# A fused attention and mixture-of-experts kernel: row counts, scatter and expert choice placed in the next step, squares at the step's end, q and k in one tile

## The chip, the cores and the metric

The kernel runs on one core of a Trainium2 chip. The metric is the device time of one execution in microseconds; the time given is the median of three runs. One further execution was taken by the hardware profiler, and all rows below come from it.

The core's engines run side by side, each in its own fixed order, and wait for one another on semaphores. PE does the matrix products (its weight loads are the row PEld), DVE and ACT work on tiles elementwise, POOL issues the indirect transfers (scatters) and SP issues the plain ones.

## What is computed

The reference computes a channel attention over four batches of 5056 tokens with 256 channels, and passes its output, as 20224 rows, through a mixture of eight experts of which each row uses one.

```python
qn = q / (np.linalg.norm(q, axis=1, keepdims=True) + 1e-06)
kn = k / (np.linalg.norm(k, axis=1, keepdims=True) + 1e-06)
s = kn.transpose(0, 2, 1) @ qn / tau            # 256 x 256 for each batch
a = softmax(s);  x = v @ a
...
logits = x @ w_gate + modality_bias[modality_id]
e_idx = np.argmax(logits, axis=1)
for e in range(E):                              # 8 experts, 256 -> 1024 -> 256
    mask = e_idx == e
    h = np.maximum(x[mask] @ w1[e], 0.0)
    out[mask] = gate_w[mask, None] * (h @ w2[e])
```

The norms run over the tokens, so a batch's `a` is known only when all of its q and k have been read. An expert's rows are known only as the routing goes on.

## The kernel before

**Steps.** The tokens are taken in steps of 512 (the last step of a batch has 448), ten to a batch, 40 in all, numbered `g`. In step `g`, three streams of pieces are merged by `_interleave`, which takes from each in proportion to its length:

- `va_pieces(g)`: the transposes `vtp` of the next step's v, their halves `vh` and `vl`, the products `xp` = v·a with their copies into `x` (L543), and then `route`;
- `kq_pieces(b + 1, s)`: loads of q and k of the next batch, halves `qs` and `ks` (L298, L299), squares and their sums for the norms (L322, L324), and the matmuls `g` = kᵀq (L343);
- `block_pieces`: one block of 512 rows of one expert, with weight halves (L722, L729), transposed rows `xtp`, `xh`, `xl`, the first layer `hp` with `hh` and `hl`, the second layer `y`, and `yo` with its scatter to the output.

Products are done in split precision: a value is kept as a high and a low half, and three products are summed. For batch 0 and the first five steps of batch 1 `g` uses whole values.

**Routing.** `route` (L547 to L608) adds the bias, finds each row's best expert as a one-hot tile `oh`, counts rows with a running sum `run`, and multiplies both with triangular and all-one matrices on PE: the three matmuls `rp` (L575 to L577). From `rp`, DVE forms the new counts `bs` (L582), each row's position `pos`, and the row numbers `pi` (L591). POOL then scatters the four tiles of `x` to their experts' places in the DRAM tensor `xs` (L454).

**Expert choice.** `pick` (L620 on) takes the counts `bs` of a step and chooses on DVE which expert has the next full block; SP loads the result `pki` into registers and uses it in the addresses of the block's weights (L701, L705) and rows (`xr`, L682). A block starts four steps after its choice (fewer after step 12); the first is chosen at step 2 and starts at step 6. There are 40 blocks, numbered by `slot`.

**What sets the order.** The program is written in the order in which the pieces are called; a scheduler then orders each engine's instructions by that and by the buffers (`p1`, `p2`, `p3`, `p4` are pools with 1 to 4 buffers per tag). Some orders are given by hand: `order(ins, others)` puts an instruction behind others of its engine, and in batch 0 the halves and squares of q and k are put behind `routed[g - 1]`, the last routing instructions of the step before. SP issues its loads in order, so a load that waits for a buffer holds those behind it. Names such as `filler1` are unused tiles that place other tiles in memory.

Of the kernel before, what the change touches and what calls it, by code (L numbers as in the profile page):

```python
# [34 lines left out]
def kernel(  # L35
# [216 lines left out]
    filled = []  # L252
    acc = {}

    def kq_pieces(b, s, behind=(), later=None):
# [11 lines left out]
        def load():  # L267
            if s == 0:
                gram[b] = ps1.tile([P, CH, C], F32, tag="y0" if b == 0 else "g", name=f"g_{b}")
                acc[b] = p1.tile([P, 2, 2 * C], F32, tag="acc", name=f"acc_{b}", bufs=2)  # L270
                if b == 0:
                    p1.tile([P, 48], F32, tag="filler2", name="filler2")
            for n, src, tag in (("q", q, "w1r"), ("k", k, "w2r")):
                if (b == 0 and s % 5 >= 2) or (b == 1 and 2 <= s < START + 2):
                    st[n] = p3.tile([P, TT, C], F32, tag=tag, name=f"{n}_{b}_{s}")
                else:
                    st[n] = p2.tile([P, TT, C], F32, tag=n, name=f"{n}_{b}_{s}")
                rows = src[b, t0 : t0 + pp * TT, :].rearrange("(p t) c -> p t c", t=TT)
                if b == 0 and s == 0:
                    st[n + "rows"] = rows  # L280
                else:
                    nc.sync.dma_start(st[n][:pp], rows)
            if b == 0 and s == 0:
                for h in range(2):
                    ts = slice(2 * h, 2 * h + 2)
                    for n in ("q", "k"):
                        nc.sync.dma_start(st[n][:, ts, :], st[n + "rows"][:, ts, :])

        def split(h):
            ts = slice(2 * h, 2 * h + 2)  # L290
            whole = s in WHOLE[b]
            more = h == 1 and (b == 0 or (b == 1 and s < START + 1))
            if not whole:
                st["q", h] = p2.tile([P, 2, 2 * C], F32R, tag="xh" if more else "qs", name=f"qs_{b}_{s}_{h}")
                st["k", h] = p2.tile([P, 2, 2 * C], F32R, tag="xl" if more else "ks", name=f"ks_{b}_{s}_{h}")
# [11 lines left out]
        def square(h):  # L307
            ts = slice(2 * h, 2 * h + 2)
            a = acc[b]
            for n, o in (("q", 0), ("k", C)):  # L310
                first = h == 0 and s == 0
                sq = a[:, :, o : o + C]
                if not first:
                    if b == 0 and s == 0 and n == "q":
                        p3.tile([P, 80], F32, tag="filler5", name="filler5", bufs=1)
                    if b == 0 and n == "k" and not filled:
                        filled.append(p3.tile([P, 48], F32, tag="filler1", name="filler1", bufs=1))
                    if b == 0 or (b == 1 and s < AHEAD):
                        sq = p3.tile([P, 2, C], F32, tag="hh" if n == "q" else "hl", name=f"sq_{b}_{s}_{h}_{n}")
                    else:  # L320
                        sq = p2.tile([P, 2, C], F32, tag="sq", name=f"sq_{b}_{s}_{h}_{n}")
                act(nc.scalar.activation(sq[:pp], st[n][:pp, ts, :], AF.Square))  # L322
                if not first:
                    dve(nc.vector.tensor_tensor(a[:pp, :, o : o + C], a[:pp, :, o : o + C], sq[:pp], ALU.add))  # L324

        def mm(h):
            for t in range(2):
                first = s == 0 and h == 0 and t == 0
                last = s == NS - 1 and h == 1 and t == 1
                for m in range(CH):  # L330
                    ms = slice(m * P, (m + 1) * P)
                    if s in WHOLE[b]:
                        seq = [(st["k"][:pp, 2 * h + t, ms], st["q"][:pp, 2 * h + t, :])]
                    else:
                        ks, qs = st["k", h], st["q", h]
                        lo = slice(C + m * P, C + (m + 1) * P)
                        seq = [
                            (ks[:pp, t, ms], qs[:pp, t, 0:C]),
                            (ks[:pp, t, ms], qs[:pp, t, C : 2 * C]),
                            (ks[:pp, t, lo], qs[:pp, t, 0:C]),  # L340
                        ]
# [16 lines left out]
    def softmax_pieces(b):  # L358
        st = {}

        def norms():
            a = acc[b]
            ns = ps2.tile([P, 512], F32, tag="aux", bufs=3, name=f"ns_{b}")
            for h in range(2):
                nc.tensor.matmul(
                    ns[:, 0:C], ones, a[:, h, 0:C], start=h == 0, stop=h == 1, skip_group_check=True
                )
            for m in range(CH):
                for h in range(2):
                    nc.tensor.matmul(  # L370
                        ns[:, C + m : C + m + 1], a[:, h, C + m * P : C + (m + 1) * P], ones[:, 0:1],
# [113 lines left out]
    def va_pieces(b, s):  # L485
# [59 lines left out]
        def route():  # L545
# [20 lines left out]
            W = TT * E  # L566
# [4 lines left out]
            if early:  # L571
# [39 lines left out]
            fetch,  # L611
        )
# [8 lines left out]
    def pick(g, slot, tail):  # L621

        nc.vector.tensor_copy(end9[:, 0:E], bases[g])
        n = 3 if tail else 2
# [16 lines left out]
        nc.vector.tensor_scalar(rem, rem, m, None, ALU.is_equal)  # L641
        nc.vector.tensor_tensor(pr[:, 0, :], rem, nxt9, ALU.mult)
        nc.vector.tensor_tensor(pr[:, 1, :], rem, eid9, ALU.mult)
# [3 lines left out]
        nc.vector.tensor_reduce(pk[:, 0:n], pr[:, 0:n, :], AX.X, ALU.add)  # L647
# [25 lines left out]
    def block_pieces(g, slot, picked, tail):  # L673
        pki, padded = picked
# [4 lines left out]
        def load_x():  # L679
            r = nc.sync.value_load(pki[0:1, 0:1], min_val=0, max_val=E * CAP)  # L680
# [14 lines left out]
        def load_w(hf):  # L695
            if hf == 0:
                st["e"] = nc.sync.value_load(pki[0:1, 1:2], min_val=0, max_val=E - 1)
# [13 lines left out]
        def split_w(ci):  # L711
            a, c = st["wr"][ci // 2]
            o = ci % 2
            if slot == 0 and ci == 0:
                p4.tile([P, 64], F32, tag="filler3", name="filler3", bufs=1)
# [36 lines left out]
        def m1(j):  # L752
# [8 lines left out]
            for i, (w, x, h) in enumerate(seq):  # L761
                nc.tensor.matmul(hp[:, 0:rows], w[:, h, fs], x[:, h, 0:rows], start=i == 0, stop=i == len(seq) - 1)  # L762
            hh = p3.tile([P, BLK], F32R, tag="hh", name=f"hh_{slot}_{j}")
            hl = p3.tile([P, BLK], F32R, tag="hl", name=f"hl_{slot}_{j}")
# [112 lines left out]
    squares = {1: [], 2: []}  # L877
    for s in BEFORE:
        if s == 0:
            run(kq_pieces(1, s))  # L880
        else:
            run(kq_pieces(1, s, lambda: routed[0], squares[s]))
    pad_rows()
    for g in range(G):
# [12 lines left out]
        streams.append(soft + (va[g + 1][0] if g + 1 < G else []) + va[g][1])  # L897
        if b + 1 < B:
            if b == 0 and s == 1:
                streams.append(list(kq_pieces(1, 2, lambda: routed[1], squares[2])))  # L900
            else:
                streams.append([f for i in (PLAN[s] if b == 0 else [s]) for f in kq_pieces(b + 1, i, routed[g - 1] if b == 0 and g > 0 else ())])
        _interleave(*streams)
        run(squares.get(g + 1, []))
# [3 lines left out]
        if s == NS // 2 and b < B - 1:  # L908
            setup_bias(b + 1, routed[g])
        n = slots_by(g)  # L910
# [87 lines left out]
```

## Time and profile before

| | |
|---|---|
| median of three runs | 1247.93 us (1247.73 to 1249.01) |
| the profiled execution's own time | 1241.93 us |
| span from first to last instruction of it | 1240.2 us |
| mean granted TensorE clock | 0.997 |
| bytes read, written | 167.06 MB, 43.43 MB |

Rows of the profile give the line of the kernel, the engine, the operation, the tile written and the tiles read, and then busy time or waits. A wait is the idle time of an engine just ahead of an instruction, with what released it. PE's clock is given as a share of full speed.

### The profile page before, as it was taken

To read this page: it belongs to the slowest core of one execution; us is meant where nothing else is said; L and a number is where in the kernel's file an instruction comes from. 1 tells how busy PE (TensorE), PEld (TensorE's weight loads), DVE (VectorE), ACT (ScalarE), POOL (GpSimd) and SP (SyncE) were. 2 spreads that over 40 slices of the span, in tenths; PEclk is the share of its full clock that TensorE was granted. 3 is DMA by queue.
4 is the path that set the end of the run, shared out by engine and by line. 5 is a ranking of instruction groups with operands and counts; after the bars stand their busy time and mean duration, and the time that the engine had idled before them with its cause. 6 is when DMAs were issued, how large, how long until landed. Compare 5 with 4: busy or idle time off the path is not lost. (4 is left out here: it accounts for less than half of the span.)

```text
span 1240.2 us, 23781 instructions
## 1 busy us (share of the span) xinstructions
PE 1215.5 (98%) x8368; PEld 1116.8 (90%) x8368; DVE 829.3 (67%) x2182; ACT 736.7 (59%) x1511; POOL 365.1 (29%) x344
## 2 busy tenths in 40 slices
PE   8989999999999999999999999999999999999997
PEld 7878898999999999998999999999899999989997
DVE  6789687767667776776677776656555665575552
ACT  6656667766666666675666666556455555545552
POOL 0053342223232333312333323322322233333121
PEclk9999999999999999999999999999999999999999
DMA  8979565455555565545555554444554454443430
GB/s 309 297 236 298 161 200 174 156 171 177 185 184 171 172 182 184 178 143 165 178 181 188 154 185 152 147 131 138 174 165 137 148 162 149 126 145 123 147 98 29
DMA packets 104177, 210.83 MB, mean 170 GB/s; under 512 B 11336, under 2 KB 52808, under 8 KB 104048
## 3 DMA queue, kind: packets, MB, share of 16 engines
q1 hardware_dynamic: 88304, 167.61, 43.5%
q0 software_dynamic: 15744, 41.61, 9.0%
q8 instruction: 67, 1.10, 0.4%
q14 instruction: 62, 0.51, 0.1%
HBM read 167.06 MB, written 43.43 MB: 170 GB/s over the span
## 5 line engine op out<-in xcount | busy, mean ns | idle before, releaser
L454 POOL DMA_INDIRECT xs<-x,pi x160 | 179.5, 1122 | 681.5 <-ACT w1h L722 302.3
L780 PE MATMUL y<-w2h,hh 128*128 128x256 f32 x1264 | 357.6, 283 | 1.8 <-issue 0.9
L780 PE MATMUL y<-w2l,hh 128*128 128x256 f32 x1264 | 352.6, 279 | 0.1
L780 PE MATMUL y<-w2h,hl 128*128 128x256 f32 x1264 | 350.9, 278 | 0.1
L766 DVE SCALAR_TENSOR_TENSOR hl<-hp,hh 128x512 fp32r<-128x512 f32 (+1 forms) x320 | 216.4, 676 | 67.8 <-ACT hh L765 61.4
L762 PE MATMUL hp<-xh,w1h 128*128 128x512 f32 (+1 forms) x640 | 254.4, 398 | 0.0
L762 PE MATMUL hp<-xh,w1l 128*128 128x512 f32 (+1 forms) x640 | 250.3, 391 | 0.0
L762 PE MATMUL hp<-xl,w1h 128*128 128x512 f32 (+1 forms) x640 | 249.9, 391 | 0.0
L780 PEld LDWEIGHTS y<-w2h,hh 128*128 128x128 f32 x1264 | 237.5, 188 | 13.1 <-ACT yo L796 1.9
L780 PEld LDWEIGHTS y<-w2l,hh 128*128 128x128 f32 x1264 | 238.0, 188 | 10.1 <-issue 0.5
L765 ACT ACTIVATE hh<-hp 128x512 fp32r<-128x512 f32 (+1 forms) x320 | 190.3, 595 | 82.6 <-PE hp L762 75.7
L780 PEld LDWEIGHTS y<-w2h,hl 128*128 128x128 f32 x1264 | 236.7, 187 | 0.5 <-DVE hl L766 0.3
L729 DVE TENSOR_TENSOR w1l<-w1r,w1h 128x512 fp32r<-128x512 f32 x160 | 110.2, 689 | 179.4 <-ACT w1h L722 171.3
L454 POOL DMA_INDIRECT out_dram<-yo,xr x158 | 171.7, 1087 | 158.0 <-ACT yo L796 121.4
L722 ACT CAST w1h<-w1r 128x512 fp32r<-128x512 f32 x160 | 100.1, 626 | 142.9 <-PE hp L762 130.1
L762 PEld LDWEIGHTS hp<-xh,w1l 128*128 128x128 f32 x640 | 120.1, 188 | 26.0
L762 PEld LDWEIGHTS hp<-xl,w1h 128*128 128x128 f32 x640 | 120.4, 188 | 14.7 <-issue 0.4
L762 PEld LDWEIGHTS hp<-xh,w1h 128*128 128x128 f32 x640 | 120.1, 188 | 12.7
L722 ACT CAST w2h<-w2r 128x512 fp32r<-128x512 f32 x160 | 101.0, 631 | 48.4 <-PE y L780 45.8
L729 DVE TENSOR_TENSOR w2l<-w2r,w2h 128x512 fp32r<-128x512 f32 x160 | 110.2, 689 | 25.3 <-ACT w2h L722 23.2
L543 ACT COPY x<-xp 128x264 f32<-128x264 f32 x160 | 61.2, 383 | 91.2 <-PE xp L539 67.5
L539 PE MATMUL xp<-ah,vh 128*128 128x264 f32 x320 | 93.1, 291 | 0.4 <-issue 0.4
(146 smaller groups left out, 1710.4 us busy)
## 6 DMA issues: line engine op xcount, KB each, us to landing
w1r<-in_moe_w_dram SPq DMA_DIRECT2D x80, 512.0 KB
w2r<-in_moe_w_dram SPq DMA_DIRECT2D x80, 512.0 KB
xr<-xs SPq DMA_DIRECT2D x38, 516.0 KB
v<-in_v_dram SPq DMA_DIRECT2D x36, 512.0 KB
q<-in_q_dram SPq DMA_DIRECT2D x35, 512.0 KB
k<-in_k_dram SPq DMA_DIRECT2D x35, 512.0 KB
xs<-x,pi POOLq DMA_INDIRECT x160
out_dram<-yo,xr POOLq DMA_INDIRECT x158
```

The costliest lines, as they stand in the source:

```text
L454: ins = nc.gpsimd.indirect_dma_start(out=dst, out_offset=bass.IndirectOffsetOnAxis(ap=idx, axis=0), in_=rows, in_offset=None, bounds_check ...
L539: nc.tensor.matmul(xp[:, 0:DE], a[:, h, t * P : (t + 1) * P], w[:, h, :], start=i == 0, stop=i == len(seq) - 1,)
L543: nc.scalar.copy(st["x"][:, t, :], xp[:, 0:DE])
L722: ins = nc.scalar.copy(hi, src).ins
L729: nc.vector.tensor_tensor(lo, src, hi.bitcast(F32), ALU.subtract)
L762: nc.tensor.matmul(hp[:, 0:rows], w[:, h, fs], x[:, h, 0:rows], start=i == 0, stop=i == len(seq) - 1)
L765: nc.scalar.activation(hh[:, 0:rows], hp[:, 0:rows], AF.Relu)
L766: nc.vector.scalar_tensor_tensor(hl[:, 0:rows], hp[:, 0:rows], 0.0, hh[:, 0:rows].bitcast(F32), ALU.max, ALU.subtract)
L780: ins = nc.tensor.matmul(y, a[:, tsl], w[:, j % 2, :], start=(j == 0 and i == 0 and t % 2 == 0), stop=(j == NJ - 1 and i == 2), skip_group ...
```

## The change

It has three parts.

1. The end of `route` becomes a function of its own, `place`: the `rp` matmuls, `bs`, `pos`, `pi` and the scatter. It is put into the stream of the next step, behind that stream's first two pieces, and the expert choice `pick` is called right behind it. A block's `picked` list is made at once and filled then. Only the last step keeps both in itself.
2. The squares of q and k and their sums are collected in a list `late` and run when the step's streams have been merged, except those of a batch's last step. The hand-written orders behind `routed` fall away for them.
3. q and k share a tile `qk` of 2 x 4 x 256 columns per partition, and their halves share `qkh` and `qkl`, so that copies, subtractions, squares and sums run over 1024 columns instead of twice 512. The two weight matrices of a half block share a tile `w` as well. `pick` forms its sums with the products, by `accum_out`, instead of by a reduction behind them.

```diff
         def split(h):
+            src = st["qk"][:pp, :, 2 * h : 2 * h + 2, :]
...
-            for n in () if whole else ("q", "k"):
-                t = st[n, h]
-                act(nc.scalar.copy(t[:pp, :, 0:C], st[n][:pp, ts, :]))
-                dve(nc.vector.tensor_tensor(
-                    t[:pp, :, C : 2 * C], st[n][:pp, ts, :], t[:pp, :, 0:C].bitcast(F32), ALU.subtract
-                ))
+            if s not in WHOLE[b]:
...
+                act(nc.scalar.copy(hi[:pp], src))
+                dve(nc.vector.tensor_tensor(lo[:pp], src, hi[:pp].bitcast(F32), ALU.subtract))
...
         def square(h):
...
-                act(nc.scalar.activation(sq[:pp], st[n][:pp, ts, :], AF.Square))
-                if not first:
-                    dve(nc.vector.tensor_tensor(a[:pp, :, o : o + C], a[:pp, :, o : o + C], sq[:pp], ALU.add))
+            act(nc.scalar.activation(sq[:pp], src, AF.Square))
+            if not first:
+                dve(nc.vector.tensor_tensor(a[:pp], a[:pp], sq[:pp], ALU.add))
...
             nc.vector.tensor_tensor_scan(rtf, keep, ohf, 0.0, ALU.mult, ALU.add)
-            if early:
+            st["routing"] = (oh, run_t, ex)
+
+        def place():
...
+            if g < first_block - 1:
                 rp = ps1.tile([P, 512], F32, tag="y0", name=f"rp_{g}")
             else:
                 rp = ps2.tile([P, 512], F32, tag="aux", bufs=3, name=f"rp_{g}")
...
-        nc.vector.tensor_scalar(rem, rem, m, None, ALU.is_equal)
-        nc.vector.tensor_tensor(pr[:, 0, :], rem, nxt9, ALU.mult)
-        nc.vector.tensor_tensor(pr[:, 1, :], rem, eid9, ALU.mult)
-        if tail:
-            nc.vector.tensor_tensor(pr[:, 2, :], rem, pr[:, 2, :], ALU.mult)
+        nc.vector.tensor_tensor(rem, rem, m.to_broadcast([P, E + 1]), ALU.is_equal)
         pk = p2.tile([P, 3], F32, tag="pk", name=f"pk_{slot}")
-        nc.vector.tensor_reduce(pk[:, 0:n], pr[:, 0:n, :], AX.X, ALU.add)
+        for i, x in enumerate((nxt9, eid9) + ((pr[:, 2, :],) if tail else ())):
+            nc.vector.scalar_tensor_tensor(
+                pr[:, 0, :], rem, 1.0, x, ALU.mult, ALU.mult, accum_out=pk[:, i : i + 1]
+            )
...
-            a = p3.tile([P, CH, FH], F32, tag="w1r", name=f"w1r_{slot}_{hf}")
-            c = p3.tile([P, JH, D], F32, tag="w2r", name=f"w2r_{slot}_{hf}")
+            w = p3.tile([P, 2, JH * D], F32, tag="w", name=f"w_{slot}_{hf}")
...
+    def placed(g):
+
+        def choose(slot, picked):
+            picked.extend(pick(g, slot, False))
+
+        return [va[g][3]] + [lambda p=p: choose(*p) for p in picks.get(g, [])]
...
-        streams.append(soft + (va[g + 1][0] if g + 1 < G else []) + va[g][1])
+        turns = va[g + 1][0] if g + 1 < G else []
+        own = soft + turns + va[g][1] + (placed(g) if g == G - 1 else [])
+        if g > 0:
+            own[2:2] = placed(g - 1)
+        streams.append(own)
+        late = []
...
+                for f in kq_pieces(b + 1, i, later=None if i == NS - 1 else late)
+            ])
         _interleave(*streams)
-        run(squares.get(g + 1, []))
+        run(squares.get(g + 1, []) + late)
```

The next rows show how PE's order changes in three places. First, PE around the counts of step 2, ahead of the first block, in the kernel before (`xp_3_0` is the first row tile of step 3, `g_1` the product for batch 1):

```order
L521 MATMUL vtp_4_0_864<-ident_79,v_4_854 128x128 x4
L539 MATMUL xp_3_0_884<-ah_0_440,vh_3_746 128x264
...
L521 MATMUL vtp_4_1_877<-ident_79,v_4_854 128x128 x4
L539 MATMUL xp_3_0_884<-ah_0_440,vl_3_747 128x264
L343 MATMUL g_1_483<-q_1_3_860,k_1_3_862 128x256 x3
L575 MATMUL rp_2_811<-oh_2_807,trim_95 128x32
L576 MATMUL rp_2_811<-run_2_809,onesb_88 128x32
L577 MATMUL rp_2_811<-run_2_809,onesb_88 128x8
L343 MATMUL g_1_483<-q_1_3_860,k_1_3_862 128x256
L539 MATMUL xp_3_1_896<-ah_0_440,vh_3_746 128x264
```

The same place in the changed kernel:

```order
L572 MATMUL rp_1_640<-run_1_619,onesb_88 128x8
L332 MATMUL g_1_413<-qk_1_3_728 128x256 x2
L528 MATMUL xp_3_0_791<-ah_0_370,vh_3_629 128x264
...
L528 MATMUL xp_3_3_815<-ah_0_370,vh_3_629 128x264
L570 MATMUL rp_2_738<-oh_2_718,trim_95 128x32
L528 MATMUL xp_3_3_815<-al_0_371,vh_3_629 128x264
...
L571 MATMUL rp_2_738<-run_2_720,onesb_88 128x32
L572 MATMUL rp_2_738<-run_2_720,onesb_88 128x8
L332 MATMUL g_1_413<-qk_1_3_728 128x256 x2
L510 MATMUL vtp_5_0_857<-ident_79,v_5_848 128x128 x4
```

The matmuls of `rp_2` stood behind the first row tile of step 3, and now its first stands behind the first matmul of the fourth; those of `rp_1` stand ahead of step 3.

Second, PE at the end of step 9, the last of batch 0, before (`hp_3_7` is the last chunk of block 3's first layer):

```order
L762 MATMUL hp_3_7_3025<-xl_3_2399,w1h_3_3_2797 128x512
L575 MATMUL rp_9_2997<-oh_9_2993,trim_95 128x32
L762 MATMUL hp_3_7_3025<-xh_3_2398,w1l_3_3_2798 128x512
L576 MATMUL rp_9_2997<-run_9_2995,onesb_88 128x32
L577 MATMUL rp_9_2997<-run_9_2995,onesb_88 128x8
L343 MATMUL g_1_483<-qs_1_9_1_2950,ks_1_9_1_2951 128x256 x12
L780 MATMUL y0_3_2752<-w2h_3_2_2725,hh_3_5_2887 128x256
```

And in the changed kernel, where `rp_9` stands in block 4:

```order
L757 MATMUL hp_4_1_2923<-xh_4_2709,w1h_4_0_2652 128x512
...
L779 MATMUL y0_3_2577<-w2h_3_3_2625,hh_3_7_2810 128x256
...
L779 MATMUL y1_3_2578<-w2h_3_3_2625,hl_3_7_2811 128x256
L570 MATMUL rp_9_2960<-oh_9_2825,trim_95 128x32
L571 MATMUL rp_9_2960<-run_9_2827,onesb_88 128x32
L572 MATMUL rp_9_2960<-run_9_2827,onesb_88 128x8
L757 MATMUL hp_4_2_3040<-xh_4_2709,w1h_4_1_2795 128x512
```

It moved behind the 12 `g` of the last q and k, three groups of `y` and two groups of `hp`.

Third, PE at the start of the first block, before:

```order
L539 MATMUL xp_5_3_1196<-ah_0_440,vl_5_991 128x264
L743 MATMUL xtp_0_0_1259<-identr_84,xr_0_1152 128x128 x4
L743 MATMUL xtp_0_1_1260<-identr_84,xr_0_1152 128x128 x4
L521 MATMUL vtp_7_0_1378<-ident_79,v_7_1124 128x128 x4
L762 MATMUL hp_0_0_1329<-xh_0_1257,w1h_0_0_1248 128x512
```

And in the changed kernel:

```order
L332 MATMUL g_1_413<-qkl_1_5_1_1418,qkh_1_5_1_1417 128x256
L332 MATMUL g_1_413<-qkh_1_5_1_1417,qkl_1_5_1_1418 128x256
L738 MATMUL xtp_0_0_1123<-identr_84,xr_0_1002 128x128 x4
L738 MATMUL xtp_0_1_1124<-identr_84,xr_0_1002 128x128 x4
L510 MATMUL vtp_7_0_1215<-ident_79,v_7_976 128x128 x3
L757 MATMUL hp_0_0_1176<-xh_0_1121,w1h_0_0_1112 128x512
```

The 24 matmuls `g` of batch 1's step 5 stand ahead of the block's row transposes `xtp` now; before, they stood inside the block.

More of the change, by code (lines that the diff above doesn't have):

```diff
@@ L251 @@
     gram = {}
-    filled = []
     acc = {}
@@ L269, in load @@
                 gram[b] = ps1.tile([P, CH, C], F32, tag="y0" if b == 0 else "g", name=f"g_{b}")
-                acc[b] = p1.tile([P, 2, 2 * C], F32, tag="acc", name=f"acc_{b}", bufs=2)
+                acc[b] = p1.tile([P, 2, 2, C], F32, tag="acc", name=f"acc_{b}", bufs=2)
                 if b == 0:
                     p1.tile([P, 48], F32, tag="filler2", name="filler2")
[L273 to L282, printed above, removed]
+            if (b == 0 and s % 5 >= 2) or (b == 1 and 2 <= s < START + 2):
+                qk = p3.tile([P, 2, TT, C], F32, tag="w", name=f"qk_{b}_{s}")
+            else:
+                qk = p2.tile([P, 2, TT, C], F32, tag="qk", name=f"qk_{b}_{s}")
+            st["qk"] = qk
+            rows = [x[b, t0 : t0 + pp * TT, :].rearrange("(p t) c -> p t c", t=TT) for x in (q, k)]
             if b == 0 and s == 0:
@@ L307, in square @@
         def square(h):
-            ts = slice(2 * h, 2 * h + 2)
+            src = st["qk"][:pp, :, 2 * h : 2 * h + 2, :]
             a = acc[b]
-            for n, o in (("q", 0), ("k", C)):
-                first = h == 0 and s == 0
-                sq = a[:, :, o : o + C]
-                if not first:
[L314 to L324, printed above, removed]
+            first = h == 0 and s == 0
+            if first:
+                sq = a
+            elif b == 0 or (b == 1 and s < AHEAD):
+                sq = p2.tile([P, 2, 2, C], F32, tag="qs", name=f"sq_{b}_{s}_{h}")
+            else:
+                sq = p1.tile([P, 2, 2, C], F32, tag="sq", name=f"sq_{b}_{s}_{h}")
+            act(nc.scalar.activation(sq[:pp], src, AF.Square))
+            if not first:
+                dve(nc.vector.tensor_tensor(a[:pp], a[:pp], sq[:pp], ALU.add))
         def mm(h):
@@ L611, in va_pieces @@
             fetch,
+            place,
         )
@@ L876 @@
     run(va[0][0])
-    squares = {1: [], 2: []}
+    squares = {s: [] for s in BEFORE if s > 0}
     for s in BEFORE:
[L879 to L882, printed above, removed]
+        run(kq_pieces(1, s, later=squares.get(s)))
     pad_rows()
+    picks = {}
+    def placed(g):
+        def choose(slot, picked):
+            picked.extend(pick(g, slot, False))
+        return [va[g][3]] + [lambda p=p: choose(*p) for p in picks.get(g, [])]
     for g in range(G):
@@ L896 @@
         soft = list(softmax_pieces(b)) if s == 0 and b > 0 else []
[L897 to L902 removed]
+        turns = va[g + 1][0] if g + 1 < G else []
[4 more added lines that the diff above has]
+        late = []
+        if b + 1 < B:
+            streams.append([
+                f
+                for i in (PLAN[s] if b == 0 else [s])
+                for f in kq_pieces(b + 1, i, later=None if i == NS - 1 else late)
+            ])
         _interleave(*streams)
[L904 removed]
+        run(squares.get(g + 1, []) + late)
         if waiting and waiting[0][0] <= g + 1 - lag(g + 1):
```

65 lines of the change are left out of this document (38 added, 27 removed).

## The prediction

> **What bounds the kernel now.** I read the page first, for the engine that is never free; then what that engine waited for; then its clock and busy time by stretches; then the timeline around its two longest waits. The first rows are the page's, by engine and in 40 slices.
>
> ```profile
> PE 1215.5 (98%) x8368; PEld 1116.8 (90%) x8368; DVE 829.3 (67%) x2182; ACT 736.7 (59%) x1511; POOL 365.1 (29%) x344
> ...
> PE   8989999999999999999999999999999999999997
> ```
>
> PE is busy for 1215.5 of 1240.2 us, and the slices show where it is not: the first hundred microseconds and the end. ACT and DVE have a third of the span and more to spare, so shorter work on them is worth nothing by itself. What can be won is PE's idle time, so the next view is PE's waits (us in total, times, longest).
>
> ```profile
> PE g L343 <- DMA k<-in_k_dram: 5.1, 2, 4.6
> PE rp L575 <- DVE sm L594: 3.3, 1, 3.3
> PE rp L575 <- DVE sm L595: 2.8, 1, 2.8
> ...
> PE xtp L743 <- DMA xr<-xs: 0.9, 1, 0.9
> PE y L780 <- issue: 0.9, 1, 0.9
> PE y L780 <- ACT yo L796: 0.8, 2, 0.6
> ```
>
> Two waits of 3.3 and 2.8 us stand at `rp`, the row-count matmuls that the change moves; the 5.1 us are the first loads of the kernel, which it leaves alone. Everything else is below 1 us. The windows (sum, then PE, PEld, DVE, ACT, POOL, clock, DMA share, GB/s) place them.
>
> ```profile
> 62.00:93.00 31.00, 27.23 (x182) 24.64 (x181) 24.93 (x104) 18.37 (x47) 18.36 (x16) 0.94 0.73 236
> 93.00:124.00 31.00, 29.96 (x209) 26.49 (x208) 28.78 (x88) 20.99 (x45) 12.01 (x8) 1.00 0.91 298
> 186.00:217.00 31.00, 28.54 (x203) 26.27 (x202) 24.74 (x45) 22.98 (x49) 6.62 (x6) 1.00 0.54 174
> 400.00:430.00 30.00, 30.00 (x214) 27.79 (x214) 22.59 (x57) 18.93 (x38) 8.52 (x8) 1.00 0.57 177
> ```
>
> A stretch from the middle is full: PE is busy for 30.00 of 30.00 us. The gain has to come from 62 to 93 and from 186 to 217, where 3.8 and 2.5 us are missing, and in the first of them the clock falls as well (0.94).
>
> **Moving the row counts, step 2.** PE's timeline around the 3.3 us:
>
> ```profile
> 70.83 1.46 PE L343 MATMUL g<-q,k 128*128 128x256 f32 x6
> 75.56 0.18 PE L575 MATMUL rp<-oh,trim 128*128 128x32 bf16 x1 [3.27 <-DVE sm L594]
> ...
> 75.87 1.09 PE L343 MATMUL g<-q,k 128*128 128x256 f32 x2
> ...
> 76.98 0.42 PE L539 MATMUL xp<-al,vh 128*128 128x264 f32 x1
> ...
> 79.18 0.39 PE L539 MATMUL xp<-ah,vl 128*128 128x264 f32 x1
> 79.40 0.29 PE L539 MATMUL xp<-ah,vh 128*128 128x264 f32 x1
> 79.53 0.28 PE L539 MATMUL xp<-al,vh 128*128 128x264 f32 x1
> ```
>
> PE stood for 3.27 us at `rp_2`, and then ran at half pace: two `g` and twelve `xp` matmuls took 79.40 - 75.87 = 3.53 us, where 14 at 0.12 to 0.13 (79.40 to 79.53) are 1.7 us. The stall therefore cost 3.3 + 1.8 = 5.1 us. In the new order 23 of the 24 `xp` matmuls of step 3 stand ahead of `rp_2`'s first matmul, some 2.8 us of work, so most of that wait is covered.
>
> The clock bears on this. After 3.27 us of idleness the pace halved here; after the 2.76 us at step 9 (below) the window's clock stays 1.00. The Trainium skill ("TensorE: Matmul & The Clock Gate", section "What's actually happening") says that the gate halves the clock after an idle window of about 3.4 us that runs free of the kernel; the trace has it after a recorded 3.27, so the measurement decides. By that rule several waits of 1 to 2 us would cost no clock, and by the rows none either, since 2.76 us cost none: the sum is the same.
>
> What is late next is the first expert block. Its rows come from the scatter of step 2, and these are the rows of that chain (POOL, SP's queue, ACT and PE):
>
> ```profile
> 78.03 0.98 POOL L454 DMA_INDIRECT xs<-x,pi  x1 [5.63 <-ACT sq_k L322]
> ...
> 83.44 0.98 POOL L454 DMA_INDIRECT xs<-x,pi  x1 [0.31 <-issue]
> ...
> 79.50 0.41 SPq L701 DMA_DIRECT2D w1r<-in_moe_w_dram  x1
> ...
> 89.57 0.14 SPq L682 DMA_DIRECT2D xr<-xs  x1
> ...
> 91.12 0.63 ACT L722 CAST w1h<-w1r 128x512 fp32r<-128x512 f32 x1
> ...
> 95.19 0.85 PE L743 MATMUL xtp<-identr,xr 128*128 128x128 f32 x8 [0.94 <-DMA xr<-xs]
> ```
>
> Step 2's scatters ran from 78.03 to 84.4, the block's rows were asked for at 89.57 and transposed from 95.19: `xtp` started 10.8 us after the last scatter. That chain starts at `rp_2`, and `rp_2` is not earlier in the changed kernel: it has 2.8 us more work ahead, and the scatters of steps 0 and 1 (four each, about 1.3 us apart) now come later too and stand ahead on POOL. Following ACT's and DVE's new orders by hand with the durations of the rows, I put step 2's scatters at 81 to 86.1 (DVE's and ACT's splits of steps 3 and 4 stand between), so `xtp` at 95.19 + 1.7 = 96.9 us. PE arrives there with more done: the 24 `g` matmuls of q|k 5 stand before the block now and stood inside it before, 24 x 0.12 = 2.9 us. So if the block's rows come no earlier than before, the early part can gain at most 2.9 us, whatever happens to the stall, and by my chain 2.9 - 1.7 = 1.2 us. Against it stand the block's first splits, which queue behind step 5's routing on ACT and DVE (about 1 us by the same orders). I take **0** for the early part and keep -2.9 and +5 (the stall's 5.1 paid a second time, at `xtp`) as ends. Most of the 5.1 us thus turns into waits at `rp_1` to `rp_4` (0.8 to 1.9 us each by hand) and at `xtp`.
>
> **Moving them, step 9.** The second wait, on ACT, DVE and PE:
>
> ```profile
> 204.59 0.63 ACT L322 ACTIVATE sq_q<-q 128x512 f32<-128x512 f32 x1 [1.17 <-DMA q<-in_q_dram]
> ...
> 208.83 0.63 ACT L322 ACTIVATE sq_k<-k 128x512 f32<-128x512 f32 x1 [3.34 <-DMA k<-in_k_dram]
> ...
> 213.93 0.38 ACT L543 COPY x<-xp 128x264 f32<-128x264 f32 x1
> ...
> 217.27 0.23 DVE L570 TENSOR_TENSOR_SCAN run<-keep,oh 128x32 bf16<-128x32 bf16 x1
> ...
> 214.14 0.40 PE L762 MATMUL hp<-xl,w1h 128*128 128x512 f32 x1
> 217.30 0.19 PE L575 MATMUL rp<-oh,trim 112*128 112x32 bf16 x1 [2.76 <-DVE sm L595]
> ```
>
> ACT stood 1.17 and 3.34 us behind squares whose loads were late, so the last copy of x ran at 213.93 and the routing ended 3.3 us later, with PE waiting. In the new order 12 `g`, three groups of 12 `y` and two groups of 6 `hp` stand before `rp_9`: at 0.12 us a matmul of 256 columns (the pitch of `xp` above) and twice that for the 512 of `hp`, 48 x 0.12 + 12 x 0.24 = 8.6 us, against an idle time of 2.76. The wait is gone: **-2.8 us**. ACT still meets the late load at a square, but what PE needs from ACT there (the `hh` of the block) is two groups ahead; if that cover failed, up to 2.8 us would return.
>
> **Moving them, all other steps.** Their three matmuls stay three, at 0.19 + 0.18 + 0.17 us overlapped, only beside the transposes of the next step. PE's small waits at `rp` (0.4 to 0.6 each) go: **-0.5 us**. The four scatters and the expert choice leave about 10 us later in a step of some 28. Blocks start four steps after their choice, so in the steady part the rows and `pki` on SP have tens of microseconds to spare; on POOL the scatters now follow the eight of a finished block, and nobody waits. `bs`, the first of the moved DVE work, waits for PE in both kernels:
>
> ```profile
> DVE bs L582 <- PE rp L577: 25.8, 21, 1.4
> ...
> ACT x L543 <- PE xp L539: 67.5, 56, 2.2
> ```
>
> Behind it on DVE stand the splits and `hl`; 1.4 us at most, hidden as now. The second row says that ACT waits for PE, not PE for ACT.
>
> **Wider operations and late squares.** The rows for 512 and 256 columns (busy, mean ns):
>
> ```profile
> L322 ACT ACTIVATE sq_k<-k 128x512 f32<-128x512 f32 x68 | 42.5, 635 | 18.1 <-DMA k<-in_k_dram 12.8 <-issue 3.9 <-ACT x L543 0.7
> L324 DVE TENSOR_TENSOR acc<-acc,sq_k 128x512 f32<-128x512 f32 x68 | 46.6, 685 | 16.5 <-ACT sq_k L322 9.4 <-issue 6.3
> L419 ACT CAST ah<-ae 128x256 fp32r<-128x256 f32 x8 | 3.2, 405 | 0.9 <-DVE ae L396 0.9
> L420 DVE TENSOR_TENSOR al<-ae,ah 128x256 fp32r<-128x256 f32 x8 | 3.4, 422 | 0.2
> ```
>
> 256 columns more cost 0.23 us on ACT and 0.26 on DVE, so 1024 take about 1.1 and 1.21 us instead of 1.27 and 1.37 in two: an estimate of 0.17 us saved for each pair. There are 80 pairs of squares and 50 of splits, so some 20 us of each engine. Neither is the bound, so I put it at **0**; if all of it lay on PE's path, it would be -20, but no PE wait in the list names these tiles. An operation that cannot be interrupted holds its engine 0.45 us longer, and the squares of a step now run as one burst of 2.2 us on ACT and 2.4 on DVE at the step's end: 0 to +9 us (two thirds of that 0.45 in each of 30 steps), taken as 0, because PE waited for ACT's `yo` only twice.
>
> **The expert choice.** Two sums come with the products now:
>
> ```profile
> L643 DVE TENSOR_TENSOR pr<-pr,eid 128x9 f32<-128x9 f32 x40 | 6.5, 162 | 0.0
> L647 DVE TENSOR_REDUCE pk<-pr 128x2 f32<-128x18 f32 x37 | 6.3, 171 | 1.1
> ```
>
> Two products and a reduction took 0.5 us; two with a sum take between 2 x 0.16 and 2 x (0.16 + 0.17). Off the path either way: **0**. Weights in one tile: the load of the first half waits for the second matrix's split as well, with two other buffers ahead: **0**.
>
> **Sum.** Profiled execution 1241.93 us (span 1240.2 and 1.7 around it): 0 - 2.8 - 0.5 = -3.3, so 1238.6. The median of the runs shown stands 6.0 us above the profiled one, so 1247.9 - 3.3 = **1244.6 us**.
>
> **Rivals.** (a) *The early wait only moves and costs more.* If scatters or the first weights (asked for at 79.50 now, about 85 by my chain of `pki_0`, which waits behind DVE's adds and splits) land later, PE waits at `xtp` or at the first `hp`. From 79.50 to the split at 91.12 were 11.6 us; 85 + 11.6 + two splits puts the first `hp` near 98, and a wait over 3.3 us halves the clock again (+1.8). This gives back 1 to 4 us: 1246 to 1249, no change. For it: the DMA engines are 0.91 busy from 93 to 124. Against: 2.8 us of work were moved ahead. (b) *Both waits vanish and the early part gains its most:* -2.9 - 2.8 - 0.5 = -6.2, 1241.7. For it: `rp_2`'s cover; against: all of POOL's, SP's and DVE's later work. (c) *Slower: the bursts of squares.* If the 2.2 us on ACT and 2.4 on DVE delay `yo`, `xh` or a weight split that PE needs next, each step loses a little; from 0.11 us a step (30 x 0.11 = 3.3) the gain is gone, and at 0.2 us a step it is 30 x 0.2 - 3.3 = +2.7, 1250.6. For it: ACT and DVE are in order, and blocks meet at step ends. Against: ACT is busy for 18.93 of 30.00 us in the middle. (d) That the order does not change as said is ruled out by the rows of the new order.
>
> **How the numbers follow.** About 0.2% (2.5 us) is what a measurement of this kernel can tell from no change. Forecast (1242.5 to 1246.5) 0.45, of which 0.10 falls within 2.5 us; (a) 0.23; (b) 0.12; (c) 0.20. Faster 0.35 + 0.12 = 0.47, same 0.33, slower 0.20. The range takes in (b) with an early gain somewhat larger than my bound and (c) up to 0.22 us a step: 1239.5 to 1251.5.
>
> **What would show it.** Right: no wait at `rp` over 2 us after step 5; no half clock after 62 us; the wait for the first `xtp` longer than 0.94; steady windows as full as 400 to 430. Wrong: PE waits for `hh`, `yo` or splits in many steps; a second stretch at half clock before 110 us; a load of q|k that `g` waits for.

## The result

| | before | changed |
|---|---|---|
| median of six runs | 1248.15 us (1246.33 to 1249.01) | 1338.98 us (1334.92 to 1353.16) |
| ratio to before, 95% interval | | 1.0734 (1.0709 to 1.0759) |
| span of the profiled execution | 1240.2 us | 1333.1 us |
| mean granted TensorE clock | 0.997 | 0.977 |

The changed kernel is 7.3% slower; the forecast was 0.3% faster, within 1239.5 to 1251.5 us. The page of the changed kernel, its first part and PE's slices:

```profile
PE 1254.9 (94%) x8368; PEld 1141.0 (86%) x8368; DVE 819.1 (61%) x2099; ACT 714.1 (54%) x1381; POOL 339.8 (25%) x344
...
PE   8979999999999999999999999999989999999997
```

PE has the same 8368 matmuls. ACT's busy time fell by 22.6 us and DVE's by 10.2, as wider operations should have it, and yet the span grew by 93 us. The slices hardly show it, because a tenth of a slice is 3 us: the loss is spread over the whole run. The window from 400 to 430 us, which was full before (30.00 us of PE, 214 matmuls), shows the rate of it:

```profile
400.00:430.00 30.00, 28.04 (x197) 25.72 (x196) 19.44 (x52) 16.37 (x33) 7.88 (x8) 1.00 0.50 161
```

17 matmuls fewer in 30 us, and every engine less busy. The three largest sums of PE's waits name no engine that would be late, and the fourth is the kernel's first load (us in total, times, longest):

```profile
PE hp L757 <- issue: 19.1, 36, 1.0
PE xp L528 <- issue: 16.8, 26, 4.8
PE y L779 <- issue: 12.9, 20, 1.1
PE g L332 <- DMA qk<-in_k_dram: 5.0, 1, 5.0
```

"Issue" means that the profile shows nothing that PE waited for. The counts, on the other hand, no longer wait in step 9 (idle time behind the last bar, 2.8 us before):

```profile
L570 PE MATMUL rp<-oh,trim 112*128 112x32 bf16 x4 | 0.8, 191 | 0.0
```

Where such an "issue" falls is seen on all engines at once. The timeline of one step, cut to the rows that matter:

```profile
443.78 0.98 POOL L443 DMA_INDIRECT xs<-x,pi  x1 [0.30 <-issue]
444.55 0.59 ACT L514 CAST vh<-vtp 128x512 fp32r<-128x512 f32 x1 [3.98 <-PE g L332]
...
445.16 0.69 DVE L515 TENSOR_TENSOR vl<-vtp,vh 128x512 fp32r<-128x512 f32 x1 [3.05 <-issue]
...
446.35 0.98 POOL L443 DMA_INDIRECT xs<-x,pi  x1 [0.30 <-issue]
446.41 0.40 PE L757 MATMUL hp<-xl,w1h 128*128 128x512 f32 x1
...
447.38 0.39 PE L757 MATMUL hp<-xh,w1l 128*128 128x512 f32 x1 [0.57 <-issue]
...
448.80 0.40 PE L757 MATMUL hp<-xh,w1h 128*128 128x512 f32 x1 [1.03 <-issue]
...
448.93 1.05 ACT L293 CAST qkh<-qk 128x1024 fp32r<-128x1024 f32 x1 [1.83 <-remote]
```

Matmuls of one `hp` group, which follow each other at 0.23 us elsewhere, start 0.97 and 1.42 us apart (446.41, 447.38, 448.80). ACT starts `vh` at 444.55, though its transposes ended at 440.98 and its own previous operation at 440.56; DVE's `vl` reads that `vh`, so DVE follows ACT, whatever name its wait carries. POOL alone keeps its pace, and what POOL does there differs from the same place before. Its timeline, first before, then changed:

```profile
403.33 0.98 POOL L454 DMA_INDIRECT xs<-x,pi  x1 [18.68 <-ACT w1h L722]
...
407.65 1.19 POOL L454 DMA_INDIRECT xs<-x,pi  x1 [0.30 <-issue]
409.81 0.98 POOL L454 DMA_INDIRECT out_dram<-yo,xr  x1 [0.97 <-ACT yo L796]
...
413.67 0.98 POOL L454 DMA_INDIRECT out_dram<-yo,xr  x1 [0.30 <-issue]
```

```profile
405.12 0.98 POOL L443 DMA_INDIRECT out_dram<-yo,xr  x1 [21.10 <-ACT yo L795]
...
408.97 1.03 POOL L443 DMA_INDIRECT out_dram<-yo,xr  x1 [0.30 <-issue]
410.31 0.98 POOL L443 DMA_INDIRECT xs<-x,pi  x1 [0.31 <-issue]
...
414.16 0.98 POOL L443 DMA_INDIRECT xs<-x,pi  x1 [0.30 <-issue]
```

Before, four scatters to `xs`, a pause of 0.97 us in which POOL waited for `yo`, and four to the output. Changed, eight in a row, 0.30 us apart, in 10.0 us: `xs` no longer waits for anything, since its positions were ready long before.

To weigh this I took PE's loss from the trace: the time from one matmul's start to the next, beyond what the same pair of matmuls usually takes. It sums to 38 us before and 131 us in the changed kernel, and the difference is the span's. (What counts as usual is a choice; another one moves the sums of many rows by some per cent, and single rows by up to 1.5 us.) In the changed kernel 98 us of it lie in 32 rows of eight scatters and the 5 us behind each (3.05 us a row), and of that most in the seventh, the eighth and just behind. Before, 32 groups of four alone lost 0.16 us each. The one unbroken row of eight to `xs` in the kernel before lost 5.0 us: it ran from 61.8 to 72.4 us and ended where my prediction had found the 3.3 us wait at step 2. Five other rows there, four to `xs` and four to the output, have no pause either; the three that took under 10.6 us lost 1.0 to 1.9 us each.

### The profile page after: what moved, and what is told of

The parts are those of the page before. It is cut to its first block, busy times and chain, and to the rows that moved or that the text cites. A ratio compares the mean times of both kernels' runs of the same rounds, so it can differ in the third digit from the quotient of the medians.

```text
span 1333.1 us, 23524 instructions
## 1 busy us (share of the span) xinstructions
PE 1254.9 (94%) x8368; PEld 1141.0 (86%) x8368; DVE 819.1 (61%) x2099; ACT 714.1 (54%) x1381; POOL 339.8 (25%) x344
## 4 chain that ended last, share of the span: by engine, by line
PE 82%; issue 10%; DVE 3%; ACT 2%; DMA 1%; POOL 1%; POOLq 0%; another core or an unknown queue 0%; SPq 0%; ACTq 0%
PE hp L757 30%; PE y L779 29%; PE xp L528 9%; PE g L332 9%; PE vtp L510 2%; PE xtp L738 2%; DMA qk<-in_k_dram 1%; POOL out_dram L443 1%; DVE acc L313 1%; DVE qkl L294 0%; DVE hl L765 0%; PE gw L404 0%; PE atp L398 0%; ACT sq L311 0%; ACT vh L514 0%
## 5 line engine op out<-in xcount | busy, mean ns | idle before, releaser
L443 POOL DMA_INDIRECT out_dram<-yo,xr x158 | 160.4, 1015 | 815.1 <-ACT yo L795 777.3
L757 PE MATMUL hp<-xl,w1h 128*128 128x512 f32 (+1 forms) x640 | 254.0, 397 | 6.8 <-issue 6.7
L779 PEld LDWEIGHTS y<-w2h,hh 128*128 128x128 f32 x1264 | 241.5, 191 | 13.8 <-issue 4.9
L724 DVE TENSOR_TENSOR w1l<-w,w1h 128x512 fp32r<-128x512 f32 x160 | 110.2, 689 | 158.9 <-ACT w1h L717 137.6
L443 POOL DMA_INDIRECT xs<-x,pi x160 | 166.8, 1042 | 136.0 <-ACT x L532 63.4
L717 ACT CAST w1h<-w 128x512 fp32r<-128x512 f32 x160 | 99.3, 621 | 185.6 <-PE hp L757 152.9
L724 DVE TENSOR_TENSOR w2l<-w,w2h 128x512 fp32r<-128x512 f32 x160 | 109.9, 687 | 41.5 <-ACT w2h L717 35.8
L717 ACT CAST w2h<-w 128x512 fp32r<-128x512 f32 x160 | 100.8, 630 | 55.1 <-PE y L779 43.8
L514 ACT CAST vh<-vtp 128x512 fp32r<-128x512 f32 x80 | 47.6, 599 | 129.5 <-PE hp L757 38.1
L528 PE MATMUL xp<-ah,vh 128*128 128x264 f32 x320 | 98.1, 307 | 12.0 <-issue 11.9
```

Source lines behind the costliest of these rows:

```text
L443: ins = nc.gpsimd.indirect_dma_start(out=dst, out_offset=bass.IndirectOffsetOnAxis(ap=idx, axis=0), in_=rows, in_offset=None, bounds_check ...
L514: cast[g] = nc.scalar.copy(st["vh"][:, h, :], tp).ins
L528: nc.tensor.matmul(xp[:, 0:DE], a[:, h, t * P : (t + 1) * P], w[:, h, :], start=i == 0, stop=i == len(seq) - 1,)
L717: ins = nc.scalar.copy(hi, src).ins
L724: nc.vector.tensor_tensor(lo, src, hi.bitcast(F32), ALU.subtract)
L779: ins = nc.tensor.matmul(y, a[:, tsl], w[:, j % 2, :], start=(j == 0 and i == 0 and t % 2 == 0), stop=(j == NJ - 1 and i == 2), skip_group ...
```

## The experiments

Theory 1: eight indirect transfers in a row on POOL hold up the other engines. Theory 2, a rival: the counts, positions and choice are in the way at the start of a step. Theory 3, another: late squares and wide operations hold ACT and DVE. All ratios are to the kernel before on the same chip, with their 95% intervals.

**A control and a pause.** The control takes the scatters out of `place` into a piece of their own, two pieces later:

```diff
+        def send():
+            x, pi = st["x"], st["pi"]
             for t in range(TT):
                 ins = scatter(
...
             own[2:2] = placed(g - 1)
+            own[4:4] = [va[g - 1][4]]
```

> The changed kernel with the four scatters to xs taken out of place into a piece of their own, two pieces later in the same stream; on POOL they still follow the four scatters of a finished block directly. It is the control for e1_pause, whose order on PE, DVE and ACT is the same. Theory 1 (eight indirect transfers in a row on POOL without a pause slow all engines: in the changed kernel 32 such rows lost 97.6 us of PE's time, 3.05 each, in the seventh, the eighth and just behind): slow like the changed kernel, 1320 to 1345 us, with 2 to 4 us of PE lost in each row of eight. Theory 2 (the counts, the positions and the expert choice stand in the way at the start of a step, on PE, DVE and SP): the same, 1330 to 1345. Theory 3 (late squares and 1024-wide operations hold ACT and DVE): the same.

Measured: 1305.53 us, 1.0436 (1.0398 to 1.0473). Slow, but below the 1320 us expected at the least: 32 rows lost 68 us, and 14 of them, which took 11.5 us or more because single transfers took longer, lost 0.2 us each. Then the same with four small operations on POOL ahead of the scatters:

```diff
         def send():
             x, pi = st["x"], st["pi"]
+            for _ in range(4):
+                ins = nc.gpsimd.iota(pause, pattern=[[1, 120]], base=0, channel_multiplier=0)
+                order(ins.ins, sent[-1:])
+                sent.append(ins.ins)
```

> e1c_close with four small iota operations on POOL between a finished block's scatters and the scatters to xs, about 0.45 us each by the 0.59 us of the iota of 160 columns, so a pause of some 2 us; nothing else differs on any engine. Theory 1: the loss of 3 us in each of 32 rows goes, 1238 to 1260 us, the clock back at 0.99 or more. Theories 2 and 3: no change against e1c_close within 5 us, since counts, squares and widths are the same.

Measured: 1245.53 us, 0.9954 (0.9930 to 0.9977). POOL's timeline shows the pause, and the window of 400 to 430 us is full again:

```profile
417.74 0.98 POOL L444 DMA_INDIRECT out_dram<-yo,xr  x1 [0.30 <-ACT sq L312]
418.73 1.14 POOL L601 IOTA filler<- 128x120 int32 x4
420.45 1.00 POOL L444 DMA_INDIRECT xs<-x,pi  x1 [0.58 <-DVE vl L516]
```

```profile
400.00:430.00 30.00, 30.00 (x213) 27.70 (x212) 21.51 (x52) 18.27 (x34) 10.22 (x12) 1.00 0.52 174
```

More work on POOL, between 417.74 + 0.98 and 420.45, took 60 us off the kernel. The order of PE, DVE, ACT and SP is the same in both traces. Theory 1 stands for the bulk, and theories 2 and 3 fall as its causes.

**Later scatters, and the change without its first part.** For the first, `own[4:4] = [...]` becomes `own.append(...)`. For the second, `place` and `pick` return to their own step:

```diff
-        own = soft + turns + va[g][1] + (placed(g) if g == G - 1 else [])
-        if g > 0:
-            own[2:2] = placed(g - 1)
+        own = soft + turns + va[g][1] + [va[g][3]]
```

> The changed kernel with only the four scatters to xs moved to the end of the next step's stream, some 15 us behind a finished block's scatters; counts, positions and expert choice stay where the change puts them. Theory 1: no row of eight without a pause is left in the steady part, 1238 to 1256 us; where the scatters come close ahead of the next block's, a pause of a microsecond is enough, as in the kernel before. Theory 2: still above 1320. Theory 3: still above 1320.

> The changed kernel without its first part: counts, positions, scatters and expert choice at the end of their own step again; late squares, q|k in one tile, 1024-wide operations and the sums in the expert choice stay. Theory 1: rows of four and four with pauses as before, so 1235 to 1256 us. Theory 2: the same, since the counts are back. Theory 3: still above 1320, since squares and widths are the change's.

Measured: 1313.79 us, 1.0519 (1.0481 to 1.0557), and 1306.81 us, 1.0429 (1.0381 to 1.0477). Both missed what I had expected from theory 1, though not the theory: later in the step, the scatters ran just behind a finished block's all the same (32 rows, 73 us lost), and without the move 23 unbroken rows in the other order, `xs` ahead of the output, lost 52 us. So neither the place of the counts nor which group comes first decides. That the kernel without the move has such rows also tells how the kernel before mostly escaped: in 28 of its 33 rows POOL paused for 0.6 to 4.0 us between the groups, mostly for ACT's `yo` by the profile. Nothing in the program asked for that pause.

**The scatter alone, in the kernel before.** The edit of `send` with `own[2:2] = [va[g - 1][3]]`, on the kernel before.

> The kernel before with one edit: the four scatters to xs stand in a piece at the start of the next step's stream, behind a finished block's four on POOL; row counts, positions, expert choice, squares and widths are those of before. Theory 1 (rows of eight indirect transfers without a pause): slower by the loss of most of 32 rows, 1290 to 1340 us, with the loss in the seventh, the eighth and just behind. Theories 2 and 3 (counts in the way; squares and widths): within 5 us of the kernel before.

Measured: 1275.67 us, 1.0206 (1.0167 to 1.0245). Less than expected, since part of the rows kept a pause: behind the first steps 22 unbroken rows of eight lost some 31 us, and six of six transfers some 11. Six are enough at full pace: the five of these that took 7.4 to 7.5 us lost 0.9 to 3.5 us, the one of 7.6 us 0.2.

**A pause in the kernel before.** The four iotas ahead of each step's scatters, chained behind POOL's last transfer; the order on PE is unchanged.

> The kernel before with four small iotas on POOL ahead of each step's scatters to xs, behind whatever POOL sent last; the order on PE, DVE and ACT is unchanged. In the first steps it parts rows of eight; later it only lengthens POOL's idle time. Theory 1: the 3.3 us at the row counts of step 2 and the half clock behind it go, since the row of eight at 61.8 to 72.4 us ended just there: 3 to 8 us faster than before. Rival, and the reading of my prediction (the routing chain is too short of time there): the wait stays at 3 us, and the time is within 2 us of before.

Measured: 1237.15 us, 0.9894 (0.9866 to 0.9921), and on another chip 1239.13 us, 0.9918 (0.9896 to 0.9940). PE at the counts of step 2, the same place as in the prediction's timeline:

```profile
70.50 1.46 PE L344 MATMUL g<-q,k 128*128 128x256 f32 x6
71.79 0.18 PE L576 MATMUL rp<-oh,trim 128*128 128x32 bf16 x1
71.86 0.18 PE L577 MATMUL rp<-run,onesb 128*128 128x32 bf16 x1
71.89 0.17 PE L578 MATMUL rp<-run,onesb 128*128 128x8 bf16 x1
71.91 0.68 PE L344 MATMUL g<-q,k 128*128 128x256 f32 x2
```

The 3.27 us and the half clock behind it are gone with a pause on POOL: `rp` follows `g` without a wait, although the order of the routing chain is what it was. My prediction had put them down to that chain. This kernel is faster than both. It gained 13.5 and 9.9 us where 3 to 8 were expected; the two profiles differ by 4.8 us only, since the profiled execution of the kernel before was 6 us below its median, and where the rest comes from is not shown.

**The length of the pause.** `range(4)` becomes `range(1)`, then `range(2)`.

> e1_pause with one iota instead of four, a pause of 0.4 to 0.6 us in place of some 2. If what counts is the pace of eight transfers (rows that took 11.3 us or more lost nothing in e1c_close, rows of 10.0 to 10.8 us lost 2.5 to 5), a row stretched by half a microsecond still loses in part: 1255 to 1300 us. If any interruption is enough: 1243 to 1250, like e1_pause.

> e1_pause with two iotas, half its pause of 1.7 us. By the rows of eight seen so far (98 of 98 that took under 10.6 us lost, 1 of 46 between 11.4 and 12) a row of 10.0 us grows to about 10.9: most rows lose still, 1255 to 1290 us, between e6_one (1292) and e1_pause (1246). If half the pause is enough: 1243 to 1250.

Measured: 1291.66 us, 1.0334 (1.0301 to 1.0367) with one, and 1248.65 us, 1.0000 (0.9984 to 1.0016) with two. A gap of 0.4 us leaves 55 us of loss in 32 rows, one of 1.1 us little in the steady part; for that one I had expected 1255 to 1290. Over sixteen traces (all but `n2_few` below), the rows of eight between 110 and 1145 us sort by how long they took from first start to last end:

| eight transfers in | rows | with over 0.8 us of PE lost | mean loss, us |
|---|---|---|---|
| under 10.6 us | 115 | 115 | 2.83 |
| 10.6 to 11.0 | 47 | 37 | 2.13 |
| 11.0 to 11.4 | 27 | 7 | 1.12 |
| 11.4 to 12 | 75 | 2 | 0.20 |
| over 12 | 260 | 26 | 0.33 |

Most of the losses above 11 us fall in the steps with a softmax (about 230, 530 to 570 and 830 to 885 us), where PE can wait for other things too, or near the end (1102 to 1116). A row that is stretched because some of its own transfers take longer (1.1 to 2 us instead of 0.98) loses no more than one with a gap: between 11.4 and 12 us, 23 rows with gaps of at most 0.44 us lost 0.24 us on average, 51 with longer ones 0.22. So the pace decides most. It is not all: from 10.6 to 11.0 us, 36 rows without a gap of half a microsecond lost 2.5 us on average, and nine with one 0.7.

**Bytes or rows.** In the changed kernel the output's scatters get 64 bytes of each row, then 16 rows instead of 128. Both kernels leave the rest of the output unwritten; the four scatters to `xs` in each row of eight stay as they are.

```diff
-                out, st["xr"].bitcast(I32)[:, t, D + 1 : D + 2], yo, ["y"], ["y"], T - 1,
+                out.rearrange("t (a c) -> (t a) c", c=16), st["xr"].bitcast(I32)[:, t, D + 1 : D + 2], yo[:, 0:16], ["y"], ["y"], T - 1,
...
+                out, st["xr"].bitcast(I32)[: P // 8, t, D + 1 : D + 2], yo[: P // 8], ["y"], ["y"], T - 1,
```

> The changed kernel with the scatters of finished blocks writing 64 bytes of each row instead of 1024, to the first sixteenth of the output; 128 rows a transfer and everything else as in the changed kernel, so the rest of each row is left out of the output. If the bytes in flight cause the loss in rows of eight, half of them are gone: below 1270 us. If it is the number of row descriptors per time: as slow as the changed kernel, 1320 to 1345, unless the transfers on POOL take another time.

> The changed kernel with the scatters of finished blocks sending 16 rows each instead of 128, so seven eighths of the output rows are left out; still eight transfers in a row without a pause. If the number of row descriptors per time causes the loss: none is left, 1235 to 1260 us. If the number of transfers without a pause does: as slow as the changed kernel, and slower pace does not explain it.

Measured: 1350.07 us, 1.0809 (1.0778 to 1.0841), and 1397.3 us, 1.1187 (1.1157 to 1.1218). Fewer bytes or fewer rows in half of the transfers bring nothing back. With 16 rows a transfer to the output took 0.93 us instead of 1.02 and the loss rose to 4.81 us a row of eight; PE's first long gap began by the sixth transfer in 13 of 32 rows, where in the changed kernel it mostly began in the seventh (24 of 32). This fits the number of transfers per time. Less to write in all eight was not tried.

**What is left of the change once the pace is mended.** `e7_all` has pauses in the first steps too; `e8_no_move_pause` is the change without its first part, with pauses; `e9_inline` is `e7_all` with `later=None`, the squares inside the streams; `x1_mixed` keeps counts and choice of steps 0 to 5 in their own step.

> e1_pause with the four iotas also between the scatters of one step and those of the next, so that the first steps have pauses too (e1_pause still lost 8.0 and 5.8 us of PE in a row of eight and a row of twelve there, and e1_pause is 5 us faster than before). Theory 1: another 5 to 12 us faster than e1_pause, 1232 to 1241 us. Rival: the early part is held by the chain of scatters, rows and first weights, and later scatters cost what the pauses bring: 1243 to 1248.

> e3_no_move (late squares, one q|k tile, 1024-wide operations, sums in the expert choice; counts, positions, scatters and choice in their own step) with four iotas on POOL ahead of each step's scatters, behind whatever POOL sent last. It is the second and third part of the change without the rows of eight in the first steps; in the steady part the finished block's scatters can still follow without a pause. Theory 1: what remains slow is only rows of eight that finish within some 11 us; where all have pauses, within 5 us of e5_before_pause (1237). Theory 3 (bursts of squares cost): 5 to 15 us slower than e7_all even where no such row is.

> e7_all with the squares inside the streams, where they stood before the change, instead of in a burst at the step's end; still 1024 wide. e7_all is 3 us slower than e5_before_pause, and its PE waits 3.3 us for ACT at the gate weights of the softmax and 4.6 us for the first block's rows. If the bursts of squares cause that difference: 2 to 5 us faster than e7_all. If the moved counts and scatters of the first steps do: the same as e7_all within 2 us.

> e7_all with counts, positions, scatters and expert choice of steps 0 to 5 in their own step, as before the change; from step 6 on they stand in the next step. e7_all reached the first block's rows at 100.2 us after a wait of 4.6 and a fall of the clock, e5_before_pause at 91.5 after 1.6; e5_before_pause waits 3.3 us at the counts of step 9, e7_all not at all. If the first block's late rows are what the change costs beside the rows of eight: 3 to 7 us faster than e7_all, at or below e5_before_pause. If the difference lies elsewhere (gate weights behind bursts on ACT, wide operations): within 2 us of e7_all.

> e5_before_pause again, on the chip of x1_mixed, so that the two can be compared: 1235 to 1241 us.

| | us | ratio to before |
|---|---|---|
| kernel before, pauses (e5, x3) | 1237.15, 1239.13 | 0.9894, 0.9918 |
| whole change, pauses (e7) | 1240.35 | 0.9928 (0.9901 to 0.9955) |
| without the first part, pauses (e8) | 1244.4 | 0.9974 (0.9961 to 0.9988) |
| whole change, squares in the streams (e9) | 1240.75 | 0.9931 (0.9909 to 0.9953) |
| whole change from step 6 on (x1) | 1241.14 | 0.9926 (0.9901 to 0.9950) |

The two kernels with pauses differ by 3.2 us on one chip and, with x1 for the change, by 2.0 on another, with intervals that overlap: the change as a whole is worth nothing that these runs can tell, or costs a little. Its parts differ. Without the first part (e8) the kernel is 3.7 us slower than e9 on the same chip, and 5.3 to 7.3 us slower than the kernel before with pauses, with intervals apart in both cases, though only one of its rows behind the first steps is unbroken and that one lost 0.2 us. By this comparison the moved counts gain about what was forecast for them, and the second and third parts cost more than that. e8 missed the 5 us around e5 that I had expected of it; e9 speaks against the bursts of squares, and wide operations, shared tiles and fallen orders were not tried apart. The waits show what is traded. The first row is from the kernel before with pauses (x3), the others from `e7_all` (PE's timeline and waits):

```profile
92.84 0.86 PE L750 MATMUL xtp<-identr,xr 128*128 128x128 f32 x8 [3.03 <-DMA xr<-xs]
```

```profile
100.17 1.22 PE L749 MATMUL xtp<-identr,xr 128*128 128x128 f32 x8 [4.64 <-DMA xr<-xs]
```

```profile
PE gw L405 <- ACT at L403: 3.3, 4, 1.1
```

The whole change wins the 3 us at the counts of step 9 and loses about as much at the first block's rows (7.3 us later, with 2.9 us more done, and a clock of 0.94 in the window from 93 to 124 us, 1.00 in x3) and at the gate weights of the softmax (3.3 us, 0.5 in x3). `e9_inline` and `x1_mixed` rule out the bursts of squares and the moved counts of the first steps as the cause of the late rows: the scatters of step 0 start at 70.1 us in `x1_mixed` and at 62.1 in x3, although `x1_mixed` has them in the same step. What makes that routing late, the fallen orders behind `routed` or the new loads, was not tried apart.

## Why the prediction was wrong

**The step that failed** is the one that priced the moved scatters at nothing: "on POOL the scatters now follow the eight of a finished block, and nobody waits." They follow four, and PE and ACT wait, with DVE behind them. I looked at POOL only for who needs its results, not for what a closed row of transfers does to the engines beside it. The runs put 98 us there. The rest of the sum, forecast at -3.3 us, came out at +2 to +3 where both kernels have pauses: the second and third parts, taken as 0, cost 5 to 7 us together in `e8_no_move_pause`. The 98 us were also no rival of mine: the slower one, bursts of squares, is not borne out by `e9_inline` (0.4 us apart from `e7_all`).

**The wait at step 2** was misread. The profile named `sm` on DVE as what ended it, and I followed the routing chain. Yet the timelines of the kernel before had this on POOL, ACT and DVE at the same time:

```profile
71.41 0.98 POOL L454 DMA_INDIRECT xs<-x,pi  x1 [0.30 <-issue]
```

```profile
71.95 0.38 ACT L543 COPY x<-xp 128x264 f32<-128x264 f32 x1 [1.75 <-PE xp L539]
73.39 0.59 ACT L525 CAST vh<-vtp 128x512 fp32r<-128x512 f32 x1 [1.06 <-PE g L343]
```

```profile
72.37 0.19 DVE L548 TENSOR_TENSOR L<-x,bsel 128x32 f32<-128x32 f32 x1 [2.28 <-issue]
```

The last of eight scatters in a row ends at 72.4. ACT copies step 2's last row tile at 71.95, although its matmuls ended at 69.14, and starts a cast at 73.39 whose transposes ended at 69.57; in `e5_before_pause` the two start at 68.96 and 69.39. DVE's 2.28 us carry the name "issue", but its operation reads that copy: DVE followed ACT, and PE followed DVE. `e5_before_pause` shows that the row was the cause: of the 3.27 us no wait is left, and the kernel is 1% faster.

**Step 9** was right: ACT behind late loads, and the counts moved out of their reach. In the changed kernel and in every kernel with its first part and pauses the wait is gone, and in the kernel before with pauses it is still 3.3 us (3.1 in x3). Without the move (e8) 1.1 us of it are left, so the other parts shorten it as well.

**The early part** had the mechanism of its limit right and the size wrong. The first block's rows do take the wait's place: `xtp` waits 4.64 us in `e7_all`, and the clock falls, which was rival (a). I had `xtp` at 96.9 us; it comes at 106.9 in the changed kernel, behind an unbroken row of twelve scatters from 70.1 to 86.0, and at 100.2 in `e7_all`. The waits of 0.8 to 1.9 us that I gave to `rp_1` to `rp_4` are at most 0.3 in `e7_all`. The pauses themselves (1.7 us each) put the scatters of step 2 back by up to 3.4 us in that kernel, so the two cannot be quite parted.

**Wider operations** were sized well, one by one. The estimates were 1.1 us on ACT and 1.21 on DVE for 1024 columns; the changed kernel has

```profile
L313 DVE TENSOR_TENSOR acc<-acc,sq 128x1024 f32<-128x1024 f32 x68 | 83.2, 1223 | 21.2 <-ACT sq L311 18.7 <-DVE acc L313 0.5 <-issue 0.2
L311 ACT ACTIVATE sq<-qk 128x1024 f32<-128x1024 f32 x68 | 72.1, 1071 | 22.1 <-DMA qk<-in_k_dram 17.6 <-DVE L L537 1.7 <-issue 1.3
```

and no time was won by it, as forecast. That it costs nothing is not borne out: `e8_no_move_pause`, with the second and third parts, is slower than the kernel before with the same pauses. No run has the wider operations or the new expert choice alone.

## What to carry to other kernels

Read the timeline of the engine that issues indirect transfers together with those of the others: where several engines start late at once, with releasers long done or with "issue" and "remote" as the only names, look for a closed row of such transfers, and do not follow the named releaser. A change that makes work ready earlier can take away a pause that nobody had planned; a microsecond of anything on the issuing engine between groups gives it back. Test a suspected cause by adding idle time on the suspect: it cost a few lines here and told what reordering left open.

## What was not expected of the hardware

Eight indirect transfers of POOL within 10.6 us cost PE 2.83 us on average, in 115 rows of 115, with ACT held as well and DVE behind it; in 11.4 to 12 us, 2 rows of 75 lost more than 0.8 us. PE's loss starts mostly with the seventh transfer, was no smaller with 64 instead of 1024 bytes a row in half of the transfers, and grew when these were shorter. DMA bandwidth is not short there: in the changed kernel's step shown, SP's queue moved nothing from 436.5 to 448 us.

By which path POOL's transfers hold the other engines stays open, but the trace narrows it. Its semaphore updates show that ACT is waiting for a signal: in the changed kernel 25 casts `vh` between 110 and 1145 us start over 1 us after both their transposes and ACT's previous operation have ended, all in or just behind an unbroken row, and each starts 0.02 us after an update of the semaphore that PE raises. In `e1c_close` there are nine such casts, and none in `e1_pause`, which differs on POOL alone. Slow transfers of instructions are not seen: in the step shown no packet of the instruction queues starts between 436 and 451.8 us, and in the rows of the changed kernel such packets took 1.13 and 0.43 us on average in the two queues, against 1.07 and 0.35 elsewhere. By the Trainium skill ("SBUF — State Buffer", section "SBUF: two separate sides") PE and ACT share no port of that memory with POOL or with transfers, so they should never wait for them there; here both start late, which puts the cause outside those ports if the rule holds. No run here shows more.
